# Values times probabilities in 64 rows: eleven matmuls a head in the first two batches of a fused attention and MLP kernel

## The chip, the cores and the metric

The kernel runs on one core of one Trainium2 chip. The metric is the device time of one execution in microseconds (us), the median of several. A core has a matrix engine (TensorE, PE in the profile, with its weight loads as PEld), VectorE (DVE), ScalarE (ACT), GpSimd (POOL), and SyncE (SP), whose queue issues nearly all transfers.

## What is computed

Four batches of attention with 12 heads each, on 448 rows of 64, with normalised queries and keys; then two chains of matrix products over all 1792 rows:

```
q_n, k_n = (rmsnorm(q, g_q), rmsnorm(k, g_k))
scores = scale * np.matmul(q_n, k_n.transpose(0, 1, 3, 2))
attn = np.exp(scores - np.max(scores, axis=-1, keepdims=True))
attn = attn / (np.sum(attn, axis=-1, keepdims=True) + 1e-09)
x = np.matmul(attn, v)                       # 12 heads side by side: 768 columns
h = np.maximum(x @ w_in, 0.0); x = (h * h) @ w_out
out = ((x @ w1) * (x @ w2) @ w3) @ w_out2
```

The weights come as 64-bit floats and are turned into 32-bit ones on the chip.

## The kernel before

TensorE multiplies rounded 32-bit numbers (F32R), so each operand is split into a high part (the rounded value, `hi`) and a low part (what is left, `lo`). A product is three matmuls: hi by hi, hi by lo, lo by hi (`mm3`, lines 397 to 399).

**Stages.** `for h in range(NH + 1)` (line 1080) runs over the 48 heads. Within one turn stand the scores of head h (`stage_qk`, lines 917 and 918, with the row maxima by DVE at lines 919 and 920), its exponentials (`stage_exp`, ACT, line 936), the transposes of the probabilities of head h-1 (`stage_t`, line 963), their split (`copy_on` line 134 on ACT, `sub_on` line 141 on DVE), the product with the values of head h-1 (`stage_v`, line 1015) and the preparation of the next heads. Between these, `fill(n)` puts matmuls of the MLP: in batch one the product of w3 and the last weight (`gen_w3o`), from batch two on the MLP of the batch before (`gen_moe`). Batch one's attention lasts to about 190 us, batch two's to about 490 us, batch three's and four's to about 945 us; after that only products are left. In batches one and two the 64-bit weights are loaded through four buffers (`raw64`), taken apart by ACT (line 321) and POOL (line 327), joined by DVE (line 334) and split.

**The values.** `v_prep` (line 983) puts the hi and the lo of a head's values side by side in `vhl`, 64 columns each, in an order that depends on whether the head is even or odd. The probabilities lie in four blocks of 128 rows: three have hi and lo apart (`ptr`), the fourth has 64 rows of hi and 64 of lo in one tile (`pte`). `stage_v` loads all 128 columns of `vhl` as weights and streams the seven probability tiles past them, into the one buffer of `ps_kv`. Half of its 128 rows then hold the values' hi times the probabilities, the other half the values' lo. ACT copies the lower or upper half to `vt` (line 1022), and DVE adds the other half to it, into the even or the odd head's half of `xf` (line 1023). When a pair of heads is complete, `stage_x` turns the sums of the exponentials (line 1004), multiplies by them (line 1029), and splits.

**What sets the order.** A scheduler orders the instructions of each engine from the order in which they are written, by priorities and its own costs, and each engine then takes its queue in that order. From head 24 on SP's order is the written one (`in_order(SP)`), and in the last part all engines' order is. Each PSUM pool has few buffers: two for scores, two for transposes, one for `kv` (which the transposed keys and, in batch one, the turned sums use too), three for `mm`.

Of the kernel before, what the change touches and what calls it, by code (L numbers as in the profile page):

```python
# [30 lines left out]
def attention_moe_kernel(  # L31
# [15 lines left out]
    nc = tc.nc  # L47
    SP, ACT, DVE, POOL, PE = (e.engine for e in (nc.sync, nc.scalar, nc.vector, nc.gpsimd, nc.tensor))
    B, P, H, C, D = q_nat.shape
    S = P * C  # L50
# [81 lines left out]
    def copy_on(eng, out, in_):  # L132
        if eng == "a":
            nc.scalar.activation(out=out, in_=in_, func=AF.Copy)  # L134
        elif eng == "g":
            nc.gpsimd.tensor_scalar(out=out, in0=in_, scalar1=1.0, scalar2=1.0, op0=ALU.mult, op1=ALU.mult)
        else:
            nc.vector.tensor_copy(out=out, in_=in_)
# [4 lines left out]
    def sub_on(eng, out, in0, in1):  # L143
        op_on(eng, out, in0, in1, ALU.subtract)
# [838 lines left out]
    def v_prep(h):  # L983
        if not (0 <= h < NH):
            return
        v = vs.pop(h)
        t = t2.tile([128, C, 2, D], F32R, name="vhl", tag="vhl")
        i = h % 2
        copy_on("v", t[:, :, i, :], v)
        sub_on(VLO_ENG[h // H], t[:, :, 1 - i, :], v, t[:, :, i, :].bitcast(F32))  # L990
        heads[h]["v"] = t
# [15 lines left out]
    def stage_v(h):  # L1007
        if not (0 <= h < NH):
            return
        d = heads.pop(h)  # L1010
        vt = d["v"].rearrange("p c a d -> p c (a d)")
        ps = ps_kv.tile([128, 512], F32, name="kv", tag="kv")
        ops = [(vt[:, kc, :], m) for kc in range(4) for m in d["pt"][kc]]
        for n, (w, m) in enumerate(ops):
            nc.tensor.matmul(ps[:, :S], w, m, start=(n == 0), stop=(n == len(ops) - 1))  # L1015
        i = h % 2
        r0, r1 = i * D, (1 - i) * D
        if i == 0:
            xf[0] = t2.tile([128, S], F32, name="xf", tag="xf")
        x = xf[0]  # L1020
        tmp = t1.tile([128, S], F32, name="vt", tag="vt")
        copy_on("a", tmp[r0:r0 + D, :], ps[r1:r1 + D, :S])
        nc.vector.tensor_tensor(out=x[r0:r0 + D, :], in0=ps[r0:r0 + D, :S], in1=tmp[r0:r0 + D, :], op=ALU.add)
# [56 lines left out]
    for h in range(NH + 1):  # L1080
        n = W3O / ((H + 1) * 6) if h <= H else (MOE / (H * 6) if h <= 2 * H else (MOE + IN) / (2 * H * 6))
# [20 lines left out]
        if h < NH:  # L1102
            v_prep(h)
# [14 lines left out]
        if even:  # L1118
            fill(n)
        stage_v(h - 1)  # L1120
        if h >= 2 * H and h % GH < 2:
            group_prep(h // GH + 1, "qk"[h % GH])
# [72 lines left out]
```

## Time and profile before

| | |
|---|---|
| median of 3 runs | 1228.66 us (1225.48 to 1230.04) |
| the profiled execution | 1230.84 us, its span 1228.8 us |
| PE busy | 1161.3 us, 95% of the span, 6150 matmuls |
| DVE busy | 855.5 us, 70% |
| ACT, POOL busy | 726.8 us, 59%; 729.0 us, 59% |
| traffic | 224.15 MB, 182 GB/s |

Columns of the rows below: an instruction has its start, its duration, engine, line, operation, output<-inputs and shape, and, in square brackets, how long its engine stood idle before it and what ended that. Matmuls are pipelined: a 448-column one is shown as 0.37 us though the next begins about 0.2 us after it, so the distance of starts is the cost. "128*112" is a weight tile of 128 rows and 112 columns.

### The profile page before, as it was taken

The numbers are of one execution on the slowest core, as the hardware profiler recorded it, in microseconds if no ns is written. First come the engines' busy times: TensorE is split into PE (matmuls) and PEld (weight loads), VectorE is DVE, ScalarE is ACT, GpSimd is POOL, SyncE is SP. The second block draws the span as 40 slices with busy tenths as digits, with TensorE's granted clock in tenths as the row PEclk, the third lists the DMA queues.
The fourth block names the chain that finished last, engine by engine and source line by source line (L and its number), as shares of the span: only waits on it lengthen the run. The fifth ranks groups of instructions, "written<-read, shape, count | busy, mean of one in ns | idle before, by whom it ended". The sixth has DMA issues, their size and how long they took to land.

```text
span 1228.8 us, 19052 instructions
## 1 busy us (share of the span) xinstructions
PE 1161.3 (95%) x6150; PEld 1038.0 (84%) x6150; DVE 855.5 (70%) x1437; ACT 726.8 (59%) x1586; POOL 729.0 (59%) x724
## 2 busy tenths in 40 slices
PE   7799999898898899999999999999999999999998
PEld 4588888787787799998989988889989999789998
DVE  5799879868986793766787566576663312887786
ACT  5799877757655655666655655565664435333352
POOL 5775535655675665765786766485764957621131
PEclk9799999999998999999999999999999999999999
DMA  7785648698887854565574656654645656243333
GB/s 219 232 252 162 193 136 280 228 291 260 272 249 228 231 157 157 153 188 153 160 216 135 191 168 192 195 168 156 181 148 160 189 158 192 86 119 107 117 103 116
DMA packets 122435, 224.15 MB, mean 182 GB/s; under 512 B 13440, under 2 KB 75104, under 8 KB 122336
## 3 DMA queue, kind: packets, MB, share of 16 engines
q1 hardware_dynamic: 120608, 220.19, 58.9%
q10 hardware_dynamic: 1728, 2.75, 0.6%
q8 instruction: 48, 0.79, 0.3%
q14 instruction: 51, 0.42, 0.1%
HBM read 157.03 MB, written 36.96 MB: 158 GB/s over the span
## 4 chain that ended last, share of the span: by engine, by line
PE 48%; DVE 9%; DMA 7%; ACT 3%; POOL 2%; issue 2%; SPq 0%; ACTq 0%; POOLq 0%; DVEq 0%
PE mm L397 12%; PE mm L398 11%; PE mm L399 11%; PE kv L1015 2%; DMA raw<-w 2%; PE pt L963 2%; DMA raw<-f_out 2%; DMA raw<-w3o 1%; POOL hl L141 1%; PE sc L917 1%; PE pt L397 1%; ACT p L936 1%; PE pt L398 1%; PE sc L918 1%; PE pt L399 1%
## 5 line engine op out<-in xcount | busy, mean ns | idle before, releaser
L141 POOL TENSOR_TENSOR hl<-raw,hl 128x384 fp32r<-128x384 f32 (+1 forms) x321 | 377.8, 1184 | 246.8 <-ACT hl L134 204.0
L134 ACT ACTIVATE hl<-raw 128x384 fp32r<-128x384 f32 (+1 forms) x405 | 225.6, 566 | 201.1 <-PE mm L399 36.8
L398 PE MATMUL mm<-x,hl 128*128 128x448 f32 (+1 forms) x640 | 236.6, 370 | 9.2 <-POOL x L141 9.2
L397 PE MATMUL mm<-x,hl 128*128 128x448 f32 (+1 forms) x640 | 240.5, 376 | 2.7 <-DVE gf L472 1.5
L399 PE MATMUL mm<-x,hl 128*128 128x448 f32 (+1 forms) x640 | 235.0, 367 | 0.7 <-POOL hl L141 0.7
L398 PE MATMUL mm<-act,hl 128*128 128x448 f32 (+1 forms) x544 | 200.0, 368 | 4.8 <-POOL act L141 3.9
L397 PE MATMUL mm<-act,hl 128*128 128x448 f32 (+1 forms) x544 | 202.3, 372 | 0.0
L399 PE MATMUL mm<-act,hl 128*128 128x448 f32 (+1 forms) x544 | 198.5, 365 | 0.0
L936 ACT ACTIVATE p<-sc,nb,rr 112x448 f32<-112x448 f32 x192 | 137.4, 720 | 95.9 <-DVE nb L920 95.8
L398 PEld LDWEIGHTS mm<-x,hl 128*128 128x128 f32 x640 | 122.2, 191 | 19.8 <-POOL x L141 11.0
L397 PEld LDWEIGHTS mm<-x,hl 128*128 128x128 f32 x640 | 122.0, 191 | 13.6 <-DVE gf L472 2.1
L399 PEld LDWEIGHTS mm<-x,hl 128*128 128x128 f32 x640 | 122.1, 191 | 10.5 <-POOL hl L141 1.0
L141 DVE TENSOR_TENSOR ptr<-pt,ptr 128x448 fp32r<-128x448 f32 x144 | 87.0, 618 | 62.8 <-ACT ptr L134 62.3
L919 DVE TENSOR_REDUCE nb<-sc 112x1 f32<-112x448 f32 x192 | 113.2, 615 | 21.6 <-PE sc L918 20.4
L327 POOL TENSOR_SCALAR raw<-raw 128x384 uint32<-128x384 uint16 (+1 forms) x110 | 80.4, 730 | 73.2 <-DMA raw<-w_in 26.2
L398 PEld LDWEIGHTS mm<-act,hl 128*128 128x128 f32 x544 | 103.2, 190 | 15.1 <-POOL act L141 6.6
L334 DVE SCALAR_TENSOR_TENSOR raw<-raw 128x384 uint32<-128x384 uint32 (+1 forms) x120 | 89.4, 750 | 36.9 <-POOL hl L141 20.1
L397 PEld LDWEIGHTS mm<-act,hl 128*128 128x128 f32 x544 | 103.4, 190 | 8.0 <-ACT p L936 0.3
L399 PEld LDWEIGHTS mm<-act,hl 128*128 128x128 f32 x544 | 103.3, 190 | 7.5
L321 ACT ACTIVATE raw<-raw 128x384 f32<-128x384 f32 (+1 forms) x120 | 70.2, 597 | 60.7 <-DMA raw<-w 27.2
L917 PE MATMUL sc<-kt,qh 128*112 128x448 f32 x192 | 76.0, 396 | 21.2 <-ACT p L936 18.3
L141 POOL TENSOR_TENSOR act<-gf,act 128x448 fp32r<-128x448 f32 x64 | 79.6, 1244 | 14.4 <-ACT act L471 7.6
(151 smaller groups left out, 2202.4 us busy)
## 6 DMA issues: line engine op xcount, KB each, us to landing
pw<-p SPq DMA_DIRECT2D x72, 392.0 KB, 4.0
raw<-f_in SPq DMA_DIRECT2D x96, 192.0 KB, 3.7
raw<-f_out SPq DMA_DIRECT2D x72, 256.0 KB, 4.4
raw<-w_in SPq DMA_DIRECT2D x32, 384.0 KB, 4.7
raw<-w_out SPq DMA_DIRECT2D x24, 512.0 KB, 5.2
raw<-w SPq DMA_DIRECT2D x32, 384.0 KB, 4.5
qt<-q_t SPq DMA_DIRECT2D x48, 224.0 KB, 3.8
raw<-f SPq DMA_DIRECT2D x56, 192.0 KB, 3.8
```

Of the source, the lines that this page charges most:

```text
L134: nc.scalar.activation(out=out, in_=in_, func=AF.Copy)
L141: (nc.vector if eng == "v" else nc.gpsimd).tensor_tensor(out=out, in0=in0, in1=in1, op=op)
L321: nc.scalar.activation(out=hi, in_=hi, func=AF.Prelu, scale=2.0**-112, alpha=-(2.0**32))
L327: nc.gpsimd.tensor_scalar(out=t[:, :n, 0], in0=low, scalar1=2.0**-13, scalar2=2.0**-14 - 0.5, op0=ALU.mult, op1=ALU.add)
L334: nc.vector.scalar_tensor_tensor(out=f[:, :n].bitcast(U32), in0=t[:, :n, 1], scalar=3, in1=t[:, :n, 0], op0=ALU.logical_shift_left, op1=AL ...
L397: nc.tensor.matmul(ps, w[:, 0, wk, :], x[0], start=(i == 0), stop=False)
L398: nc.tensor.matmul(ps, w[:, 0, wk, :], x[1], start=False, stop=False)
L399: nc.tensor.matmul(ps, w[:, 1, wk, :], x[0], start=False, stop=(i == last))
L917: nc.tensor.matmul(o[j], d["qh"][:, c * P:(c + 1) * P], d["kt"], start=True, stop=False)
L919: nc.vector.tensor_reduce(out=nb[:, j:j + 1], in_=o[j], axis=AX.X, op=ALU.max, negate=True)
L936: nc.scalar.activation(out=p, in_=o[j], func=AF.Exp, scale=d["rq"][:, c:c + 1], bias=nb[:, j:j + 1], accum_out=sm[:, i, c:c + 1],)
L963: nc.tensor.transpose(to[:kn, c * P:(c + 1) * P], d["p"][c][:, k0:k0 + kn], one)
```

## The change

In heads 0 to 23 `vhl` always has hi in the first 64 columns. `stage_v` no longer loads 128 columns but 64: first the hi columns with the seven tiles, then the lo columns with the four tiles that hold the hi of the probabilities (of `pte`, hi and lo together). All eleven accumulate in the same 64 rows, and ACT copies these straight to the head's half of `xf`. The product of the two lo parts is left out for three blocks. Heads 24 to 47 stay as they were.

```diff
         i = h % 2
+        i = i if h >= 2 * H else 0
         copy_on("v", t[:, :, i, :], v)
...
-        ops = [(vt[:, kc, :], m) for kc in range(4) for m in d["pt"][kc]]
+        plain = h < 2 * H
+        if plain:
+            ops = [(vt[:, kc, :D], m) for kc in range(4) for m in d["pt"][kc]]
+            ops += [(vt[:, kc, D:], d["pt"][kc][0]) for kc in range(4)]
+        else:
+            ops = [(vt[:, kc, :], m) for kc in range(4) for m in d["pt"][kc]]
         for n, (w, m) in enumerate(ops):
-            nc.tensor.matmul(ps[:, :S], w, m, start=(n == 0), stop=(n == len(ops) - 1))
+            nc.tensor.matmul(ps[:D if plain else 2 * D, :S], w, m, start=(n == 0), stop=(n == len(ops) - 1))
...
         x = xf[0]
+        if plain:
+            copy_on("a", x[r0:r0 + D, :], ps[:D, :S])
+            return
         tmp = t1.tile([128, S], F32, name="vt", tag="vt")
```

The scheduler orders the queues anew. On PE, around the product of the sixth head of batch one (`kv`, between MLP products `mm` and the next head's scores `sc`), before:

```order
L399 MATMUL mm<-act,hl 128x384
L1015 MATMUL kv<-ptr,vhl 128x448 x6
L1015 MATMUL kv<-pte,vhl 128x448
L397 MATMUL mm<-act,hl 128x384
L398 MATMUL mm<-act,hl 128x384
L399 MATMUL mm<-act,hl 128x384
L917 MATMUL sc<-kt,qh 112x448
L918 MATMUL sc<-kt,ql 112x448
```

and with the change:

```order
L399 MATMUL mm<-act,hl 128x384
L1021 MATMUL kv<-ptr,vhl 64x448 x6
L1021 MATMUL kv<-pte,vhl 64x448
L1021 MATMUL kv<-ptr,vhl 64x448 x3
L1021 MATMUL kv<-pte,vhl 64x448
L397 MATMUL mm<-act,hl 128x384
L917 MATMUL sc<-kt,qh 112x448
L918 MATMUL sc<-kt,ql 112x448
```

Four matmuls came in behind the seven, and two products that stood between them and the scores stand later.

On DVE, in the same head, from the scale of the maxima (`nb`) over the next head's maxima to the pair's product (`xf<-kv,xf`), before:

```order
L920 TENSOR_TENSOR nb<-nb,rr 112x2
L889 SCALAR_TENSOR_TENSOR ql<-qt,gg,qh 128x448
L334 SCALAR_TENSOR_TENSOR raw<-raw_1638 128x384
L138 CAST vhl<-v 128x4x64
L840 TENSOR_REDUCE ss<-qn 112x16
L919 TENSOR_REDUCE nb<-sc 112x1
L1023 TENSOR_TENSOR xf<-kv,vt 64x448
L919 TENSOR_REDUCE nb<-sc 112x1
L141 TENSOR_TENSOR ptr<-pt,ptr 128x448
L920 TENSOR_TENSOR nb<-nb,rr 112x2
L1029 TENSOR_TENSOR xf<-kv,xf 128x448
```

and with the change:

```order
L889 SCALAR_TENSOR_TENSOR ql<-qt,gg,qh 128x448
L920 TENSOR_TENSOR nb<-nb,rr 112x2
L840 TENSOR_REDUCE ss<-qn 112x16
L138 CAST vhl<-v 128x4x64
L919 TENSOR_REDUCE nb<-sc 112x1 x2
L920 TENSOR_TENSOR nb<-nb,rr 112x2
L1038 TENSOR_TENSOR xf<-kv,xf 128x448
L141 TENSOR_TENSOR ptr<-pt,ptr 128x448 x3
```

The add is gone from between the two maxima, their scale comes ahead of the split of the next transposes, and a low part of the queries (`ql`) now stands ahead of the scale instead of behind it.

## Rows read from the trace of the kernel before

**Rows 1.** Stretches: start:end, length, then busy of PE, PEld, DVE, ACT, POOL, clock, DMA.

```profile
60.00:100.00 40.00, 38.18 (x229) 33.39 (x227) 37.22 (x65) 35.86 (x78) 29.14 (x32) 1.00 0.77 234
100.00:130.00 30.00, 27.54 (x172) 25.13 (x171) 28.02 (x55) 26.99 (x61) 18.70 (x23) 1.00 0.55 163
...
280.00:310.00 30.00, 25.49 (x135) 22.77 (x134) 26.93 (x44) 23.18 (x49) 18.30 (x20) 0.94 0.84 262
310.00:340.00 30.00, 25.95 (x129) 22.29 (x129) 28.61 (x42) 17.79 (x37) 19.71 (x20) 0.94 0.84 279
...
370.00:400.00 30.00, 25.49 (x127) 22.17 (x125) 21.08 (x37) 17.47 (x40) 17.45 (x21) 0.83 0.77 225
```

**Rows 2.** Timeline of PE: the values' product of one head in batch one.

```profile
104.61 1.40 PE L1015 MATMUL kv<-ptr,vhl 128*128 128x448 f32 x6
105.85 0.37 PE L1015 MATMUL kv<-pte,vhl 128*128 128x448 f32 x1
```

**Rows 3.** Timeline of PE: every idle time shown from 49 to 200 us.

```profile
56.21 0.60 PE L398 MATMUL mm<-x,hl 128*128 128x384 f32 x1 [2.71 <-POOL x L141]
60.91 0.44 PE L399 MATMUL mm<-x,hl 128*128 128x384 f32 x1 [0.67 <-POOL hl L141]
70.81 0.45 PE L917 MATMUL sc<-kt,qh 128*112 128x448 f32 x1 [1.07 <-ACT p L936]
108.15 0.46 PE L917 MATMUL sc<-kt,qh 128*112 128x448 f32 x1 [1.02 <-ACT p L936]
119.09 0.45 PE L917 MATMUL sc<-kt,qh 128*112 128x448 f32 x1 [1.32 <-ACT p L936]
142.39 0.46 PE L917 MATMUL sc<-kt,qh 128*112 128x448 f32 x1 [1.38 <-ACT p L936]
144.76 0.57 PE L1004 MATMUL kv<-ident,rsw 112*128 112x112 f32 x4 [0.29 <-DVE xf L1023]
154.43 0.46 PE L917 MATMUL sc<-kt,qh 128*112 128x448 f32 x1 [0.87 <-ACT p L936]
165.58 0.46 PE L917 MATMUL sc<-kt,qh 128*112 128x448 f32 x1 [0.96 <-ACT p L936]
190.57 0.58 PE L1004 MATMUL kv<-ident,rsw 112*128 112x112 f32 x4 [0.68 <-DVE xf L1023]
```

**Rows 4.** Groups by shape: the add on DVE, from 100 to 190 and from 200 to 420 us (count, busy, mean ns).

```profile
L1023 DVE TENSOR_TENSOR xf<-kv,vt 64x448 f32<-64x448 f32 x8 | 4.8, 606 | 0.1
...
L1023 DVE TENSOR_TENSOR xf<-kv,vt 64x448 f32<-64x448 f32 x9 | 5.5, 616 | 0.1
```

**Rows 5.** Waits of PE (200 to 420 us) and of POOL (to 424): total, times, longest.

```profile
PE mm L1004 <- DVE gf L472: 4.8, 2, 2.6
...
PE kv L1015 <- DVE pte L141: 0.2, 1, 0.2
...
POOL rsw L949 <- PE mm L399: 1.2, 1, 1.2
```

**Rows 6.** The chain that ended last: start, us, what; and the 24th product's row.

```profile
364.39 4.48 DMA raw<-w
...
424.68 0.48 PE sc L917
...
436.12 1.42 PE kv L1015 x7
...
L1015 PE MATMUL kv<-ptr,vhl x35: 362/366/370, 489.8 to 585.4; 128*128 128x448 f32 x35
```

**Rows 7.** Weight loads of 128 and 64 columns, and two neighbouring 384-column matmuls.

```profile
L1015 PEld LDWEIGHTS kv<-ptr,vhl 128*128 128x128 f32 x48 | 8.9, 188 | 0.6
...
L963 PEld LDWEIGHTS pt<-ident,p 112*64 112x64 f32 x32 | 3.1, 111 | 0.1
...
68.18 0.33 PE L398 MATMUL mm<-x,hl 128*128 128x384 f32 x1
68.35 0.33 PE L399 MATMUL mm<-x,hl 128*128 128x384 f32 x1
```

## The prediction

> **What bounds the kernel now.** I read the table of stretches first. In batch one PE is busy 38.2 of 40 us and 27.5 of 30, and DVE 37.2 of 40 and 28.0 of 30 [rows 1]: the two run neck and neck, and the change gives to the one what it takes from the other. In batch two PE falls to 25.5 and 26.0 of 30 us while DVE stands at 26.9 and 28.6, transfers at 0.84 and the clock at 0.94, then 0.83 [rows 1]. So a share of the whole span tells nothing here; each stage has to be priced for itself.
>
> Next the timeline of PE, for its idle times. From 49 to 200 us it shows ten, 10.97 us together [rows 3]. The most regular kind is a score matmul that waits for ACT's exponentials to leave the score banks; five of these (1.02, 1.32, 1.38, 0.87, 0.96 us) come within four microseconds behind the values' product of a head, as at 108.15 behind 104.61 and 105.85 [rows 2, 3]. Two more (0.29 and 0.68) wait for the very add that is removed, because it holds the only `kv` bank [rows 3]. Then the waits from 200 to 420 us: PE's come to 20.2 us in eleven rows, nearly all ended by DVE, ACT or POOL, the first being 4.8 us for DVE [rows 5]. Nobody waits long for PE: POOL 1.2 us, DVE not in any row [rows 5]. Last the chain: it goes through transfers of weights and their conversion (4.48 us at 364.39), enters PE at 424.68 and stays on PE, with the product of a head on it at 436.12 [rows 6]. So batch one is a balance of PE and DVE, batch two up to 424 us belongs to DVE, POOL and the transfers, and from there to the end PE sets the time.
>
> **The change, part by part.**
>
> *Four more matmuls a head, on PE.* Six starts take 105.85 - 104.61 = 1.24 us, so 0.207 us each [rows 2]; four cost 0.83 us, in 24 heads 19.9 us. No row shows such a matmul with 64 weight columns. Below, the nearest row is the load of 64 columns, 0.111 us against 0.188 for 128 [rows 7]; were a matmul as cheap as its load, eleven would take 1.22 us against the 1.45 of seven now, a gain of 0.23 a head. [...] I take 0.207, because the number of columns that stream stays 448, and two 384-column matmuls start 0.17 us apart, closer than a load of 0.188 takes [rows 7]: loads run beside the matmuls and don't pace them.
>
> [...]
>
> *No add, on DVE.* 4.8 us in eight, 5.5 in nine, so 0.61 each [rows 4], in 24 heads 14.7 us. ACT's copy keeps its shape and only writes elsewhere: nothing. The `kv` bank is free one DVE operation earlier, but 0.83 us of matmuls later.
>
> *Batch one, heads 0 to 11.* PE gets 12 x 0.83 = 10.0 us. What hides it: the first product lies ahead of an idle time of 2.71 us that POOL ends, so 0.83 goes there; the five idle times behind a product are each longer than 0.83, and what ends them (DVE's maxima, then ACT) doesn't depend on that product: 4.15. Of the two waits for the add, 0.97 us, I count half as gone, since ACT's copy is still waited for: 0.5. Left 10.0 - 0.83 - 4.15 - 0.5 = 4.5 us. If that cover is gone the term is 10.0; if all ten idle times go with it, 10.0 - 10.97 = -1.0.
>
> *Batch two up to 424 us, heads 12 to 20.* Nine products, 7.5 us, against 20.2 us of idle PE [rows 5] and a chain that lies elsewhere: nothing, at most 2.5 for the first three, before the conversion falls behind. DVE is the full engine from 280 to 340 us [rows 1], with three adds in it: -1.8. If all nine counted it would be -5.5. And since PE arrives at this stage with idle time ahead, about a quarter of batch one's 4.5 is taken up there: -1.1.
>
> *From 424 us, heads 21 to 23.* These products are on the chain, the 24th begins at 489.8 [rows 6]: 3 x 0.83 = 2.5, at least 0.
>
> *What moves.* The transposed probabilities and `vhl` are held 0.83 us longer; the next users stand behind the product in PE's queue anyway: nothing beyond the above. The two products that now stand behind the scores make the scores come earlier and give part of the cover back. On DVE the low part of the queries now stands in some heads ahead of the scale that the exponentials wait for; an operation of this width is about one add, 0.61 us, and the five heads with the idle time could lose it: up to 3.0. The add gone from between two maxima does the reverse. On SP the loads of heads and weights change places by a few. I set these against each other at nothing, with 3 us either way.
>
> **Sum:** 4.5 - 1.8 - 1.1 + 2.5 = +4.1 us. Against the profiled execution, 1230.84 us (its span 1228.8), that is 1234.9. This execution is 2.2 us above the median of 1228.66, and I carry the difference to the median: 1232.8.
>
> **The rivals.**
>
> *PE takes it all (slower).* The idle times don't shrink but move, since the heads' scores, exponentials and transposes go round PE in a ring: what ends an idle time was itself started later. Then 10.0 + 2.5 + 2.5 = +15.0, 1243.7 us. For it: PE's 95% in batch one. Against it: the five idle times end by work that began before the product.
>
> *DVE's backlog decides (faster).* Its place is batch two: if each add that goes brings the joins of weights and the exponentials forward, all nine count. It decides from the point where 5.5 us there outweigh batch one's rest. With all idle times of batch one used up: -1.0 - 5.5 + 2.5 = -4.0, 1224.7 us. [...] For it: DVE's 28.6 of 30 us. Against it: the chain from 348 to 424 us has conversions of DVE on it, but no such add.
>
> *The loads pace PE (faster).* Then the product shrinks by 0.23 us: 12 x -0.23 - 1.8 - 3 x 0.23 = -5.3, 1223.4 us. Against it stand the 384-column matmuls.
>
> That the change doesn't do what it says is excluded by the order: eleven matmuls, and no add.
>
> **How the numbers follow.** Forecast 0.59, with its own range 1227 to 1239; PE takes it all 0.20; DVE's backlog 0.14; loads 0.07. About 0.5%, 6.1 us, is what a measurement of this kernel tells from no change. Above 1234.8 lie most of the first rival and a quarter of the forecast, 0.34; below 1222.5 about half of the two fast rivals, 0.11; the rest 0.55. The range leaves out the upper half of the first rival and the lower half of the fast ones: 1223 to 1242.
>
> **What would show it.** Right: the values' matmuls with 64 rows still start 0.207 us apart; the idle times behind them in batch one shrink to under 0.6; the end of batch one comes about 4 us later; at 424 us the distance is smaller, at 490 larger again, and from there constant. Wrong: idle times as long as before behind longer products (first rival), an earlier 424-us mark (second), or starts clearly closer than 0.2 us (third).

## The result and the profile after

The changed kernel takes 1243.63 us, the median of 6 runs (1240.16 to 1247.9), against 1229.35 us (1225.48 to 1230.28, 6 runs) of the kernel before: a ratio of 1.0126, 95% interval 1.0104 to 1.0149. It is slower by about 14 us. The forecast was 1232.8 us with a range of 1223 to 1242; the time lies above the range, and nearly on the 1243.7 us of the first rival. The profiled execution took 1243.71 us, its span 1241.7.

The page of the changed kernel, busy time, share and instructions of each engine:

```profile
PE 1180.1 (95%) x6246; PEld 1044.4 (84%) x6246; DVE 839.1 (68%) x1413; ACT 726.3 (58%) x1586; POOL 727.1 (59%) x724
```

PE has 96 matmuls and 18.8 us more than before, and the span grew by 12.9 us: only 5.9 of the 18.8 went into idle time. DVE has 24 instructions and 16.4 us less. Stretches of the changed kernel (start:end, length, busy of PE, PEld, DVE, ACT, POOL, granted clock, transfers, GB/s), to be laid beside [rows 1]:

```profile
60.00:100.00 40.00, 38.32 (x235) 33.66 (x236) 34.83 (x66) 36.00 (x80) 29.09 (x32) 1.00 0.76 234
100.00:130.00 30.00, 27.35 (x170) 23.65 (x170) 22.30 (x43) 26.76 (x59) 17.17 (x24) 1.00 0.55 163
280.00:310.00 30.00, 26.06 (x132) 22.64 (x131) 23.20 (x38) 20.82 (x46) 17.89 (x20) 0.93 0.82 251
310.00:340.00 30.00, 26.75 (x134) 22.89 (x132) 27.17 (x45) 21.07 (x46) 17.70 (x18) 0.94 0.82 266
370.00:400.00 30.00, 24.59 (x113) 20.80 (x112) 20.69 (x36) 16.21 (x38) 17.36 (x21) 0.83 0.74 219
```

DVE fell from 28.0 to 22.3 of 30 us at 100 us and from 28.6 to 27.2 at 310. It has time to spare, and PE is no less busy for it: it is as busy as before, but part of that is the longer products. The granted clock is the same.

The product of one head in the changed kernel on PE's timeline, and its weight loads by shape (count, busy, mean ns):

```profile
106.44 1.37 PE L1021 MATMUL kv<-ptr,vhl 128*64 128x448 f32 x6
107.65 0.37 PE L1021 MATMUL kv<-pte,vhl 128*64 128x448 f32 x1
107.86 0.77 PE L1021 MATMUL kv<-ptr,vhl 128*64 128x448 f32 x3
...
L1021 PEld LDWEIGHTS kv<-ptr,vhl 128*64 128x64 f32 x216 | 29.5, 137 | 13.0 <-DVE ptr L141 0.6 <-issue 0.2
L1021 PEld LDWEIGHTS kv<-ptr,vhl 128*128 128x128 f32 x144 | 27.0, 188 | 2.3
```

Six starts take 107.65 - 106.44 = 1.21 us, 0.202 each, against 0.207 in [rows 2]. A load of 64 columns takes 137 ns instead of 188 [rows 7], and the matmuls start no closer for it: loads don't pace them here, the third rival is out, and the price of 0.83 us a head was right.

**Where the time comes in.** As a mark I take in each head the start of the product's first matmul on the edge rows (`kv<-pte`, 105.85 in [rows 2]). Marks of the changed kernel against before, each from the timeline of one execution; one_join and held_change below have the same queues up to head 6 and still differ by up to 2.7 us there, so less than that means nothing:

| mark | before, us | after | against before |
|---|---|---|---|
| head 3 | 94.69 | 95.08 | +0.4 |
| head 6 | 129.57 | 132.12 | +2.6 |
| head 7 | 139.94 | 145.38 | +5.4 |
| head 11, the last of batch one | 186.64 | 194.07 | +7.4 |
| head 15 | 278.96 | 288.26 | +9.3 |
| head 20 | 410.03 | 421.89 | +11.9 |
| head 21 | 437.17 | 446.46 | +9.3 |
| head 23, the last of batch two | 490.80 | 502.24 | +11.4 |
| end of the span | 1228.8 | 1241.7 | +12.9 |

Some 7 us come in batch one, 4 in batch two, 1.5 later. The forecast for these places was +4.5, then +1.6 at 424 us, then +4.1. Now the idle times of PE, on the timeline of the changed kernel from 100 to 200 us, all of 0.9 us and more (in square brackets the idle time ahead and what ended it):

```profile
102.89 0.60 PE L963 MATMUL pt<-ident,p 112*128 112x112 f32 x4 [0.95 <-DVE ptr L141]
...
121.68 0.46 PE L917 MATMUL sc<-kt,qh 128*112 128x448 f32 x1 [1.29 <-ACT p L936]
134.94 0.46 PE L917 MATMUL sc<-kt,qh 128*112 128x448 f32 x1 [1.65 <-ACT p L936]
159.60 0.46 PE L917 MATMUL sc<-kt,qh 128*112 128x448 f32 x1 [1.38 <-ACT p L936]
188.70 0.45 PE L917 MATMUL sc<-kt,qh 128*112 128x448 f32 x1 [1.59 <-ACT p L936]
```

The waits of [rows 3] for the add are gone. The waits for the exponentials are fewer, but those that are left last about as long as the longest of their kind there (1.32 and 1.38) or longer, behind products that are longer too. What stood ahead of the one at 134.94 shows on the chain of waits of the changed kernel (start, us, what):

```profile
128.60 0.62 POOL kx L873
129.24 3.86 DMA kn<-k_nat
133.13 1.06 ACT qn L838
134.18 0.71 ACT p L936 x2
134.90 0.04 issue
134.94 0.46 PE sc L917
```

And ACT's own timeline there, of the changed kernel:

```profile
129.32 0.67 ACT L884 ACTIVATE qh<-qt,gg 128x448 fp32r<-128x448 f32 x1
133.13 1.06 ACT L838 ACTIVATE qn<-kn 112x1024 f32<-112x1024 f32 x1 [3.14 <-DMA kn<-k_nat]
134.09 0.71 ACT L936 ACTIVATE p<-sc,nb,rr 112x448 f32<-112x448 f32 x1
```

The square of the next group's keys stands in ACT's queue ahead of the next exponentials, and it waits 3.14 us for its load; the exponentials, and behind them PE, wait with it. Between heads 6 and 7 the distance to before grows from 2.6 to 5.4 us. In the kernel before the two squares of this group, of the queries and of the keys, come at 128.10 and at 138.44, neither of them waits, and between them the exponentials go through:

```profile
128.10 1.04 ACT L838 ACTIVATE qn<-qn 112x1024 f32<-112x1024 f32 x1
129.69 0.73 ACT L936 ACTIVATE p<-sc,nb,rr 112x448 f32<-112x448 f32 x1 [0.55 <-DVE nb L920]
...
138.44 1.04 ACT L838 ACTIVATE qn<-kn 112x1024 f32<-112x1024 f32 x1
```

So the question for the experiments is whether the time comes from the change itself or from the new order that the scheduler gave everything around it.

### The profile page after: what moved, and what is told of

It reads as the page before. It is cut to its first block, busy times and chain, and to the rows that moved or that the text cites. A ratio compares the mean times of both kernels' runs of the same rounds, so it can differ in the third digit from the quotient of the medians.

```text
span 1241.7 us, 19210 instructions
## 1 busy us (share of the span) xinstructions
PE 1180.1 (95%) x6246; PEld 1044.4 (84%) x6246; DVE 839.1 (68%) x1413; ACT 726.3 (58%) x1586; POOL 727.1 (59%) x724
## 4 chain that ended last, share of the span: by engine, by line
PE 52%; DVE 15%; DMA 13%; ACT 8%; POOL 6%; issue 5%; SPq 1%; ACTq 0%; POOLq 0%; DVEq 0%
PE mm L397 12%; PE mm L398 12%; PE mm L399 11%; PE kv L1021 3%; DMA raw<-w 3%; PE pt L963 3%; ACT p L936 3%; DMA raw<-w_out 2%; POOL hl L141 2%; DVE raw L334 2%; DVE vhl L138 2%; DMA raw<-f_out 2%; DVE nb L919 2%; DMA raw<-w_in 2%; PE sc L917 2%
## 5 line engine op out<-in xcount | busy, mean ns | idle before, releaser
L472 DVE TENSOR_TENSOR gf<-mm,r 128x448 f32<-128x448 f32 x64 | 39.7, 620 | 72.2 <-ACT r L468 72.0
```

Source lines behind the costliest of these rows:

```text
L472: nc.vector.tensor_tensor(out=gf, in0=ps, in1=r, op=ALU.mult)
```

## The experiments

Ratios are to runs of the kernel before taken beside each kernel, with 95% intervals. Code is shortened; "..." marks what is left out.

### The sizes of the parts, in the order that the scheduler gives

**seven_64**: the changed kernel with the seven matmuls of the hi columns only, and no add.

```diff
-            ops += [(vt[:, kc, D:], d["pt"][kc][0]) for kc in range(4)]
```

> The changed kernel without the last four matmuls of a head: seven matmuls of 64 rows, no add (the lo part of the values is left out of batches one and two). PE's work is that of before, DVE has 14.7 us less. If the four matmuls are the loss, this is no slower than before: 1225 to 1229 us. If DVE's backlog is worth what the second rival says, 1221 to 1225. If the scheduler's new order of the queues is the loss, it stays above 1235.

Measured: 1228.26 us, ratio 1.0009 (0.9985 to 1.0033). Taking the add away alone gives nothing that shows.

**ring_add**: the kernel before with four more matmuls of 128 columns in each head of batches one and two, and the add kept.

```diff
+        if h < 2 * H:
+            ops += [(vt[:, kc, :], d["pt"][kc][0]) for kc in range(4)]
```

> The kernel before, add and 128 rows kept, with four more matmuls behind the seven of each head of batches one and two (the hi of the probabilities is counted twice there). PE has 19.9 us more, DVE nothing less. If every matmul in the heads' ring is paid, +14 to +18 us, 1243 to 1247, and the removed add was worth 0 to 4. If the idle times behind the product take them up, as forecast, +4 to +7, 1233 to 1236, and the loss of the change lies in its order.

Measured: 1248.89 us, 1.0183 (1.0158 to 1.0209), +21.6 us for 19.9 us of matmuls.

**fill_96**: the kernel before with about as much more work for PE, but among the MLP's products and not in the heads.

```diff
...
+            if more["due"] >= 1:
+                more["due"] -= 1
...
+                nc.tensor.matmul(ps, w[:, 1, wk, :], x[1], start=False, stop=False)
```

> The kernel before, with as much more work on PE but outside the heads: 57 matmuls of 384 columns among the MLP products of batch one and 48 of 448 among those of batch two (lo by lo, 9.9 us in each batch). If only PE's throughput counts, it costs what the four matmuls in the ring cost, about +14 us. If the ring counts and products between the heads fall into PE's idle times, it costs clearly less: +3 to +8 us, 1232 to 1237.

Measured: 1260.63 us, 1.0272 (1.0246 to 1.0298): +33.3 us for 19.9. Of the runs in the scheduler's order this told the most: the loss is 13.4 us more than the work that was put in, which this work alone doesn't explain; at the old order (held_fill, below) the same matmuls cost 5.9 us. Where the work stands (in a ring with the exponentials or not) is not the cause, as the first rival has it.

**batch1_only** and **batch2_only**: the change in heads 0 to 11, or in heads 12 to 23 alone.

```diff
-        plain = h < 2 * H
+        plain = h < H               # the other kernel: H <= h < 2 * H
```

> The change in heads 0 to 11 alone. In the changed kernel's trace the product of head 11 begins 7.5 us later than before. If that lateness is carried to the end, 1236 to 1238; if batch two's idle PE takes it up, 1230 to 1233 (a quarter taken up, as forecast: 1235).

> The change in heads 12 to 23 alone. With batch one alone at +8.3 us, the two add up if batch two alone costs +5 to +7, 1232 to 1235. By the forecast's terms for batch two (+0.7) it would be no change, 1227 to 1229.

Measured: 1235.62 us, 1.0075 (1.0045 to 1.0104), and 1239.74 us, 1.0082 (1.0053 to 1.0111). Each half costs some two thirds of the whole. The sum, 1.0157 with 0.004 either way, lies above the whole's 1.0126 but isn't clear of it, and in the marks the halves add up: +5.2 and +6.0 us at head 23, against +11.4 of the whole. The add and the matmuls, parted by seven_64 and ring_add, don't: 1.0009 and 1.0183 make 1.0192, clear of 1.0126.

### The order held

The next kernels keep the order of the kernel before: a table of the names of its instructions, one list for each engine, and between neighbours of a list a dependence that only orders them in their queue. The four new matmuls stand right behind the seven, and the add is left out of the list.

```diff
+    def hold():
...
+        by_name = {i.name: i for i in nc.cur_bb.bb.instructions}
+        for names in ORDER.values():
+            for a, b in zip(names, names[1:]):
+                tc.add_manual_dep(by_name[b], a, why, reason="held order")
...
     chain()
+    hold()
```

Set side by side by operation and tile, without the added matmuls and the adds, the traces of before and of the changed kernel have at least 105 instructions of PE, 105 of DVE, 92 of ACT, 39 of POOL and 38 of SP in another place; held_change has none. What the holding by itself does wasn't tried: no kernel of before with its own order held was run. Line numbers in the rows of these kernels are higher by 5 to 9.

**held_change**: the full change with this order on all five engines.

> The changed kernel with the order of before held on all five engines: the four matmuls stand right behind the seven, the add is taken out, and every other instruction keeps the place in its queue that it had before the change. If the scheduler's new order gave the cover away (it put two products behind the scores), the idle times behind the values' product now take up the four matmuls as forecast: +2 to +6 us, 1230 to 1234. If every matmul among the heads is paid whatever the order, +12 to +16, 1240 to 1244.

Measured: 1230.0 us, 1.0011 (0.9996 to 1.0026), against 1.0126 with the scheduler's order. Of the 14 us, 12 or more belong to the order.

Where the forecast's cover went can be read in the stretch from 100 to 187 us, first of before, then of the changed kernel, then of held_change:

```profile
100.00:187.00 87.00, 80.96 (x501) 73.72 (x500) 75.34 (x157) 72.98 (x167) 43.58 (x56) 1.00 0.55 165
```

```profile
100.00:187.00 87.00, 81.28 (x497) 70.05 (x496) 63.55 (x132) 65.90 (x151) 40.24 (x53) 1.00 0.52 152
```

```profile
100.00:187.00 87.00, 86.22 (x540) 76.53 (x539) 72.94 (x154) 74.33 (x171) 44.17 (x56) 1.00 0.57 172
```

In the same 87 us PE starts 501 matmuls before, 497 in the changed kernel though its heads have eleven, and 540 at the old order. With the old order PE's idle time falls from 6.0 to 0.8 us; with the new one it stays at 5.7. The waits for the exponentials in this stretch (total, times, longest) fall at the old order from

```profile
PE sc L917 <- ACT p L936: 5.5, 5, 1.4
```

in the kernel before to

```profile
PE sc L926 <- ACT p L945: 0.7, 2, 0.6
```

in held_change, and are 4.3 us in three waits in the changed kernel. That is the cover that the forecast counted on, and all of it is there. These rows are of one execution, and held_change's took 1226.1 us, 3.9 less than its median, so its marks look better than its time.

**held_seven** and **held_ring**: at the old order, the change without its four added matmuls (as in seven_64); and the kernel before with the four added and the add kept (as in ring_add).

> Seven matmuls of 64 rows and no add (the lo part of the values is left out of batches one and two), with the order of before held on all engines. The removed add alone, at a fixed order. If it is worth something that the new order hid, -2 to -5 us, 1223 to 1226; if DVE's time there is worth nothing, 1227 to 1229.

> The kernel before with four more matmuls of 128 rows in each head of batches one and two (the hi of the probabilities is counted twice there) and the add kept, in the order of before on all engines. The matmuls alone, at a fixed order. If the order was the loss, +3 to +8 us, 1231 to 1236; if PE's work among the heads is paid, +17 to +21, 1245 to 1249, as with the order that the scheduler made for it.

Measured: 1222.94 us, 0.9951 (0.9934 to 0.9968), and 1237.48 us, 1.0069 (1.005 to 1.0089). At one order the add is worth 6 us, and the added matmuls cost 8.5 us of their 19.9; the sum, +2.5, agrees with held_change's +1.4 within its interval of 1.8 either way. In the scheduler's orders the same two gave +1.1 and +22, and together +15.

**held_fill**: fill_96's added matmuls at the old order of all the rest.

> The kernel before with the 105 extra matmuls among the MLP products (19.9 us of PE), in the order of before on all engines, each extra one beside the product it belongs to. With the scheduler's own order this was +33 us. The four matmuls in the ring at a fixed order were +9. If at a fixed order PE's idle times take up about half wherever the matmuls stand, +7 to +12, 1235 to 1240; if only those behind a head's seven fall into idle times, +15 to +20, 1243 to 1248.

Measured: 1233.32 us, 1.0048 (1.0031 to 1.0066): 5.9 us, where the scheduler's order made it 33. PE had some 11 to 14 us of room for 20 us of work wherever it was put in.

### Which queue

Now the full change with the old order on some engines alone. An engine that isn't held takes what the scheduler gives it under the constraints of the others, and that is not its order in the changed kernel: in free_act at least 62 instructions of ACT move, there 92.

```diff
-ORDER = {'Pool': ..., 'Activation': ..., 'DVE': ..., 'SP': ..., 'PE': ...}
+ORDER = {'PE': ...}                                  # hold_pe; the others likewise
```

> The changed kernel with PE's order of before held (four matmuls behind the seven) and the other four engines' order left to the scheduler. With all five held it was the time of before, with none +14 to +16 us. If the two products that moved behind the scores on PE are the loss, this is 1229 to 1232 us; if the loss lies in DVE's, ACT's, POOL's or SP's queue, 1238 to 1244; if it takes both, between.

> The changed kernel with DVE's order of before held (the adds taken out), the other engines free. If the loss is the low part of the queries ahead of the scale of the maxima, and what else DVE does in another order, this is 1229 to 1233 us. If PE's order is the loss, 1238 to 1244.

> The changed kernel with the order of before held on DVE, ACT, POOL and SP, and PE's left to the scheduler. The complement of the run with PE's order alone: if PE's order is the loss, 1238 to 1244 us; if the others', 1229 to 1232.

> The changed kernel with the order of before held on PE, DVE, POOL and SP, and ACT's left to the scheduler. With all five held it was the time of before, with PE alone free +4 us, with DVE alone held +13, with PE alone held +20: the loss lies in ACT's, POOL's or SP's queue. If ACT's (its copies of the transposes and its exponentials behind other work), 1236 to 1244 us; if not, 1229 to 1232.

> The changed kernel with the order of before held on PE, DVE, ACT and POOL, and SP's left to the scheduler. If the loss lies in the order of the loads (two fewer loads of the second batch's weights were issued by 190 us in the changed kernel), 1236 to 1244 us; if not, 1229 to 1232.

> The changed kernel with the order of before held on PE, DVE, ACT and SP, and POOL's left to the scheduler. If the loss lies in POOL's queue, 1236 to 1244 us; if not, 1229 to 1232.

> The changed kernel with ACT's order of before held and the other four free. If ACT's order is the loss, 1229 to 1233 us; if it is not, or if the loss is spread over several queues, 1236 to 1244.

| held | us | ratio | interval |
|---|---|---|---|
| none: the change | 1243.63 | 1.0126 | 1.0104 to 1.0149 |
| PE alone (hold_pe) | 1248.16 | 1.0166 | 1.0132 to 1.0199 |
| DVE alone (hold_dve) | 1240.91 | 1.0103 | 1.0065 to 1.014 |
| ACT alone (hold_act) | 1234.48 | 1.0048 | 1.0023 to 1.0072 |
| all but ACT (free_act) | 1239.16 | 1.0069 | 1.0049 to 1.0089 |
| all but PE (hold_all_but_pe) | 1231.21 | 1.0031 | 1.0008 to 1.0054 |
| all but POOL (free_pool) | 1229.51 | 0.9996 | 0.9972 to 1.002 |
| all but SP (free_sp) | 1224.68 | 0.9965 | 0.9944 to 0.9987 |
| all (held_change) | 1230.0 | 1.0011 | 0.9996 to 1.0026 |

ACT's order matters most: holding it alone takes away 10 of the 15 us, and freeing it alone costs 7. Holding it also changes what the scheduler gives the others (39 moved instructions of POOL become 27, 105 of PE 81), so the 10 us aren't all ACT's. PE's own order, though no engine has more moved instructions, is worth 2 or 3 us when all others are held, too little to be told from nothing, and holding PE or DVE alone gives nothing that these intervals can show. SP's order is better left to the scheduler: free_sp is the full change, and it beats both kernels by 4 us and more. Why was not settled, nor whether the kernel before would gain as much from that order of SP. In the traces its heads are level with held_change's within 0.9 us up to head 14, 1.4 to 2.9 us behind at heads 15 to 18, and 2.1 to 3.2 ahead from head 19 on.

What ACT's order does can be seen in free_act, on ACT's timeline and on PE's:

```profile
156.61 0.53 ACT L142 ACTIVATE xf<-kv 64x448 f32<-64x448 f32 x1
160.71 0.54 ACT L329 ACTIVATE raw<-raw 128x384 f32<-128x384 f32 x1 [3.57 <-DMA raw<-w_in]
161.15 0.96 ACT L142 ACTIVATE ptr<-pt 128x448 fp32r<-128x448 f32 x2
```

```profile
162.39 1.70 PE L971 MATMUL pt<-ident,p 112*128 112x112 f32 x8 [2.09 <-DVE ptr L149]
```

```profile
162.39:166.00 3.61, 3.61 (x15) 3.56 (x16) 2.19 (x6) 3.17 (x8) 1.75 (x3) 0.53 0.14 36
```

The conversion of a weight tile waits 3.57 us for its transfer, two copies of transposes that were ready stand behind it, and PE idles for 2.09 us. The last row is the stretch behind that: the granted clock is 0.53 in it, and two products of 384 columns start 0.32 us apart there (164.24 and 164.56), where ahead of the stop two start 0.17 apart (159.50 and 159.67). From head 8 to head 9 the marks of this kernel go from +1.6 to +5.2 us, more than PE idled. ACT's waits for transfers, from 60 to 195 us (total, times, longest), first in free_act, then in hold_act, the changed kernel and held_change, a fence each:

```profile
ACT raw L329 <- DMA raw<-w_in: 6.0, 4, 3.6
...
ACT qn L846 <- DMA qn<-q_nat: 1.4, 2, 1.2
```

```profile
ACT raw L326 <- DMA raw<-w_in: 0.4, 1, 0.4
```

```profile
ACT qn L838 <- DMA kn<-k_nat: 4.2, 2, 3.1
...
ACT raw L321 <- DMA raw<-w_in: 1.2, 1, 1.2
```

```profile
ACT raw L330 <- DMA raw<-w_in: 2.8, 4, 1.7
```

The changed kernel and free_act, with the scheduler's order on ACT, have 5.4 and 8.2 us of such waits with single ones of 3.1 and 3.6; hold_act and held_change, with the old order there, have 0.6 and 2.8, with none over 1.7. hold_pe and hold_dve, where ACT is free, have 7.9 and 8.8 us (2.3 and 2.5 the longest). The sum is no measure of the time: with 8.2 us free_act is faster than the changed kernel with 5.4.

In batch two the same waits part the kernels as well. From 200 to 490 us they come to 50 us before, 53 in held_change and 48 in hold_act, but to 64 in the changed kernel, 59 in free_act, 66 in hold_dve and 69 in hold_pe. Two thirds of the growth from before to the changed kernel are in one row, here of before and of the changed kernel:

```profile
ACT raw L321 <- DMA raw<-w_out: 9.7, 6, 3.1
```

```profile
ACT raw L321 <- DMA raw<-w_out: 18.6, 10, 3.3
```

All this is a reading beside dozens of other instructions that moved. So the last two runs move one, in batch one; in batch two none was moved.

### One instruction

Both are held_change with one instruction of ACT put earlier in its queue, and nothing else.

**one_square**: the square of the keys, the instruction that stood ahead of the exponentials in the changed kernel. ACT's queue:

```diff
 L847 ACTIVATE qn<-qn 112x1024
+L847 ACTIVATE qn<-kn 112x1024
 L945 ACTIVATE p,sm<-sc,nb,rr 112x448 x2
...
 L822 ACTIVATE nt<-nt 112x32
-L847 ACTIVATE qn<-kn 112x1024
 L143 ACTIVATE osb<-mm 128x384
```

> The change with the order of before held on all engines, but with one instruction of ACT moved: the square of the keys of one group, at 137.87 us in the held kernel, now stands directly ahead of the two exponentials that began there at 129.00 us. Its load was issued at 125.77 us and took 4.5, so the square should wait until about 130.3 and let the exponentials begin at about 131.2, 2.2 us later than in the held kernel. If one ACT instruction that waits for a load hands its wait on to PE for good, the heads behind that place start about 2 us later, still do so at the end of batch one, and the kernel takes 1232 us against the held kernel's 1230.0. If PE's queue has other work to take up such a stop, the heads are level with the held kernel again two or three heads later, and the time stays at 1230.

**one_join**: one conversion of a weight tile, put ahead of three copies.

```diff
+L330 ACTIVATE raw_2422<-raw_2422 128x384
 L143 ACTIVATE kt<-kv 128x448
 L143 ACTIVATE ptr<-pt 128x448
...
-L330 ACTIVATE raw_2422<-raw_2422 128x384
 L945 ACTIVATE p,sm<-sc,nb,rr 112x448 x2
```

> As the one before, but with another single instruction of ACT moved: the conversion of a weight tile (raw from raw) at 139.56 us in the held kernel now stands ahead of the three copies of transposes that began there at 135.34 us. Its load was issued at 135.96 us and took 3.3 to 3.6, so ACT should stand for about 4 us with the copies behind it, as it does for 3.57 us in the kernel with ACT's queue left free. If such a stop is handed on for good, heads from there on start about 4 us later and the time is about 1234 us (1.0045). If it is taken up by other work, the heads are level again before the end of batch one and the time stays at 1230 (1.001).

ACT's timeline of one_square, then the only idle time of PE in that kernel between 128 and 136 us:

```profile
127.18 1.05 ACT L847 ACTIVATE qn<-qn 112x1024 f32<-112x1024 f32 x1
131.28 1.06 ACT L847 ACTIVATE qn<-kn 112x1024 f32<-112x1024 f32 x1 [3.06 <-DVE ss L849]
132.24 0.71 ACT L945 ACTIVATE p<-sc,nb,rr 112x448 f32<-112x448 f32 x1
```

```profile
133.10 0.45 PE L926 MATMUL sc<-kt,qh 128*112 128x448 f32 x1 [2.61 <-ACT p L945]
```

And ACT's timeline of one_join, then PE's wait behind it:

```profile
142.60 0.54 ACT L330 ACTIVATE raw<-raw 128x384 f32<-128x384 f32 x1 [4.83 <-DMA raw<-w_in]
143.04 0.53 ACT L143 ACTIVATE kt<-kv 128x448 fp32r<-128x448 f32 x1
```

```profile
143.62 2.09 PE L1030 MATMUL kv<-ptr,vhl 128*64 128x448 f32 x6 [2.66 <-ACT kt L143]
145.51 0.57 PE L1030 MATMUL kv<-pte,vhl 128*64 128x448 f32 x1
...
147.38 0.42 PE L406 MATMUL mm<-act,hl 128*128 128x384 f32 x1
```

The stretches right behind PE's idle time, first of one_square, then of one_join (columns as in [rows 1], the clock third from the end):

```profile
133.00:137.00 4.00, 3.90 (x28) 3.72 (x28) 2.85 (x8) 4.00 (x11) 1.34 (x3) 1.00 0.40 133
```

```profile
143.60:147.40 3.80, 3.78 (x12) 2.32 (x13) 3.30 (x8) 3.58 (x9) 0.00 (x0) 0.57 0.08 30
```

The square waited 3.06 us, and the last thing that it waited for was not its load but DVE's sum of the square ahead of it (`ss`), since both squares write the same tile. That I had left out of the expectation, which said 2.2; it makes the stop longer and changes nothing else. The marks against held_change:

| mark | one_square | one_join |
|---|---|---|
| head 5 | +0.4 | +2.7 |
| head 6, ahead of the stop | -0.1 | +2.3 |
| head 7 | +2.8 | +5.8 |
| head 9 | +2.8 | +7.1 |
| head 11 | +2.8 | +7.0 |
| head 13 | +1.7 | +5.4 |
| head 20 | +1.7 | +5.6 |
| head 23 | +1.7 | +4.3 |

The level ahead of the stop differs from run to run (+2.3 in one_join); the step is what counts. In one_square ACT stops for 3.06 us, PE idles for 2.61, and every head of the rest of batch one comes 2.9 us later: PE's queue makes up for hardly any of it. In one_join the step is 4.7 us, but that it equals ACT's stop of 4.83 is chance. PE still had work in front of it at first and idled for only 2.66. Then the granted clock fell (0.57 in the 3.8 us behind, where one_square kept 1.00), and the product's eleven matmuls took 3.76 us (143.62 to 147.38) against 2.22 in held_change (138.47 to 140.69), 1.5 us more. So this stop of ACT cost PE twice: 2.66 us of idle time, and behind it, at a clock of 0.57, these 1.5 us. What is given back in batch two, 1 to 3 us by the marks, is about what two executions differ by. In time: 1231.58 us, 1.0029 (1.0006 to 1.0051), and 1230.52 us, 1.0027 (1.0002 to 1.0053). Against held_change's 1.0011 that is 2 us each, which is less than these intervals can part from nothing. So that one stop of ACT delays the heads for good is shown in the traces through batch one; whether the 2 and 4 us expected from that are left at the end, or nothing, isn't.

In one_square ACT kept to the order of its queue: exponentials that began at 129.00 us in held_change began at 132.24, behind a square that waited 3.06 us.

## Why the prediction was wrong

**The bound, and the price.** The price of a matmul (0.207 forecast, 0.202 measured) and the exclusion of the loads held. That batch one is a balance of PE and DVE is true of the busy time in [rows 1], but PE is what binds there: from 100 to 187 us held_change keeps PE busy for 86.2 of 87 us and DVE, less its adds, for 72.9.

**Batch one, +4.5.** The cover that it counted is real: at the old order the waits behind the products shrink from 5.5 to 0.7 us. The mark of head 11 comes 1.9 us earlier there, less than two executions differ by; in the changed kernel it was +7.4. "What ends them doesn't depend on that product" is true of the old queue only; the scheduler filled the queue anew.

**Batch two to 424 us, -2.9.** Held_change goes from -1.9 at head 11 to -4.9 at head 20, that is -3.0. That it meets the forecast shows little: at the end of the span this execution is 4.7 us ahead of before's, where the medians put held_change 1.4 behind. In the changed kernel it is +4.4 instead. ACT's waits for transfers grow here, as shown above. Another thing that moved there is DVE's joins behind POOL's splits (200 to 424 us, of before and of the changed kernel):

```profile
DVE raw L334 <- POOL hl L141: 15.8, 11, 3.1
```

```profile
DVE raw L334 <- POOL hl L141: 27.9, 20, 3.3
```

It is 17.7 us in held_change. What these 12 us are worth on the way to the end was not tried.

**From 424 us, +2.5.** Held_change goes from -4.9 at head 20 to -3.8 at head 23: +1.1. In one execution of each, this can't be told from 2.5.

**What moves, nothing with 3 us either way: the step that failed.** The sum of the other terms was +4.1 us, and held_change, which is the change without this term, measured +1.4 (at most +3.2). That the two are so near is in part luck: the add was forecast at 0.5 + 1.8 = 2.3 us and held_seven measured 6.0, and the matmuls at 4.5 + 0.5 - 1.1 + 2.5 = 6.4 and held_ring measured 8.5, so that two errors set each other off. The term itself, the ratio of the change less that of held_change, is 0.0115 of 1229 us, 14 us, with some 3 either way. I had listed two of its effects. The low part of the queries ahead of the scale did happen: on the chain of the changed kernel a `ql` of 0.59 us, at 120.11, lies between the maximum and the scale, ahead of the idle time at 121.68. But I had priced single neighbours that changed places on DVE and SP, each at the length of the instruction itself, and had not gone down ACT's queue. There an instruction put ahead of others before its input had come cost not only its own length but the wait that it brought along: 3.1 us of ACT beside a length of 1.06 in the changed kernel, 3.6 beside 0.54 in free_act. I also set the gains and losses against each other, as if an order had equal chances to be better or worse. Of the kernels here whose order the scheduler chose anew for added or changed work, none was faster than its twin at the old order: 1.0126 to 1.0011, 1.0009 to 0.9951, 1.0183 to 1.0069, 1.0272 to 1.0048.

**The first rival** gave the right number, 1243.7, for another reason. What it said of the trace came true: idle times as long as before behind longer products. But its mechanism, that cover in a ring can't exist, falls with held_change, where the same products in the same ring cost 1.4 us with the add's gain in it, and with held_ring, where they cost 8.5 of their 19.9 without it. What came 14 us dear is the order of the queues. **DVE's backlog**, the second rival, is half right at the old order: held_seven's 6 us for the add (3.9 to 8.1 by its interval), where I had counted 1.8 for batch two and named 5.5 as the most. Where those 6 us arise wasn't traced. Half of the two fast rivals was put below 1222.5 us, though their sums are 1224.7 and 1223.4: that counted also on a gain from the clock in batch two, which no run shows. From 370 to 400 us the clock is 0.83 before [rows 1] and 0.83 in the changed kernel, and the shortest median of all kernels here is held_seven's 1222.94 us.

**The signs named in advance.** Starts 0.207 us apart: yes. Idle times under 0.6 us: not in the changed kernel (1.29 to 1.65), but in held_change (0.6 the longest). Batch one's end 4 us later: 7.4. A smaller distance at 424 us: no, the largest, 11.9.

**What stays open.** With ACT held alone, 1.0048 is left, some 4 us above held_change: the other queues together, not taken apart further. How much of the 14 us comes through stops of ACT is not measured; two single stops could not be told in the time. Of batch two's share only the marks and the waits are known. Four runs lay outside all that was expected of them by more than 3 us: fill_96, batch2_only and hold_pe above, free_sp below. For fill_96 held_fill shows the order as the reason; for the others none was found. And the 1.5 us after head 23, where both kernels have the same code, lie within what two executions differ by.

## What to carry to other kernels

Where a scheduler orders the queues, price a change twice: the change at the old order, and the order itself. The second can be the larger (14 us against 1.4 here), it is measured by holding the old order with dependences that only order, and it is looked for on the engine that other engines' short steps go through, at each instruction there that waits for a transfer: what stands behind it, and is it ready? Parts that were timed each in an order of its own need not add up: without the add +1 us, with the matmuls +22, together +15.

## What the runs showed that I had not expected

- The same 20 us of matmuls cost 33 us or 6, by the order of everything else (fill_96, held_fill).
- A stop of ACT of 3.06 us reached the last head of the batch, four heads on, with 2.9 us of it left, though PE's queue holds products of the MLP too: they stood behind the score matmul that waited (133.10), and the next two began at 133.59 and 133.76. PE idled 2.61 us at once.
- Behind stops of 2.66 us (one_join) and 2.09 us (free_act) of PE the granted clock fell to 0.57 and 0.53 for some 3.7 us; behind one of 2.61 us (one_square) it stayed at 1.00.
- A load of 64 columns takes 137 ns where one of 128 takes 188: half the columns, 73% of the time.
- The full change with the old order on four engines and the scheduler's own on SP takes 1224.68 us, 0.9965 (0.9944 to 0.9987). At the old order alone the change gains nothing (1.0011), so this gain may be that of SP's order rather than of the change.
